# Sliding-window attention into a SwiGLU block: transposes moved from TensorE to DMA, denominators by ones columns, first two FFN tiles interleaved

## The chip, the cores and the metric

One core of a Trainium2 chip. The metric is the device time of one execution, in microseconds (us). A run counts as fast when it is within 1.5% of the fastest of the same kernel. The granted clock is the share of TensorE's full clock that the profile records as granted. "SP" is the SyncE queue, which issues DMAs in program order; "ACT" is ScalarE, "DVE" VectorE, "PE" TensorE, "POOL" GpSimd.

## The reference

```python
def attention(q, k, v):                    # each [8 batches, 8 heads, 576, 64]
    scores = q @ k.T / sqrt(64)
    # query i sees keys i-63 .. i only
    attn = softmax(where((rel >= 0) & (rel < 64), scores, -1e9))
    return attn @ v

def reference(q, k, v, w_gate, w_val, w_out):
    x = attention(q, k, v)                 # as [4608 tokens, 512 channels]
    g = x @ w_gate                         # [512, 1536]
    return (silu(g) * (x @ w_val)) @ w_out # [1536, 512]
```

## The kernel before

The 4608 tokens are cut into 9 tiles t of 512. A tile has 4 units: unit u = 4t + p is a pair of heads, and needs loads of q, k and v, transposed queries and keys (channels on partitions), scores, exponentials, a mask, products with the values, and a division by the softmax denominators. A stage w = 4t + s does a quarter of the FFN of tile t (three gate/value blocks, and a quarter of the output projection of tile t-1) and, from w = 4, attention work some units ahead. Per unit:

```python
def casts(u):                  # GpSimd: f32 -> bf16
    nc.gpsimd.tensor_copy(q_b[:], ...); nc.gpsimd.tensor_copy(k_b[:], ...)
    nc.gpsimd.tensor_copy(vb[0:64, p, :, 0:64], v_f[0:64]); ...
def transposes(u):             # TensorE, then copies out of PSUM
    for i, x in enumerate((q_b, k_b)):
        for c in range(4):
            nc.tensor.transpose(tp[:, i, P * c:P * c + P], x[:, c, :], identb[:])
    nc.scalar.copy(qT[:], tp[:, 0, :])
    nc.vector.tensor_copy(kb[0:64, p, :, 0:64], kt[0:64])        # block-diagonal keys
    nc.vector.tensor_copy(kb[64:128, p, :, 64:128], kt[64:128])
def products(u):
    for j in range(-1, 8):
        nc.tensor.matmul(o_ps[:, lo:hi], vb, Ef[:, e0:e0 + hi - lo], ...)   # channels x queries
    for c in range(2):                                                      # denominators
        nc.tensor.matmul(d_ps[:], bones[:], E[:, :, c, :], ...)
    nc.vector.reciprocal(r[:], d_ps[:])                                     # 128 x 512
    nc.vector.tensor_mul(xT[t][:, p, :], o_ps[:], r[:])
```

The even part of the schedule:

```python
    for w in range(NU):
        # ... (w < 4 is the start)
        gate_value(t, 3 * s)
        products(w + 4)
        gate_value(t, 3 * s + 1)
        transposes(w + 5)
        project(t - 1, s, ps_o, "o")      # ends with a store by SP
        load(w + 8)                       # all loads by SP
        casts(w + 6)
        scores(w + 5)
        gate_value(t, 3 * s + 2)
```

Loads of a unit are split where a tile crosses a batch (576 is not a multiple of 512): 6 DMAs a unit at the first and last tile, 12 at the other even tiles, up to 20 at odd tiles, each with 256-byte rows.

The softmax here doesn't subtract the row's maximum and nothing guards it: scores larger than these inputs give would overflow.

## Time and profile before

| | before |
|---|---|
| median of 3 runs | 470.54 us (470.15 to 472.04) |
| PE, DVE busy | 78%, 72% |
| period of a stage in the even part | 11.5 us |
| period of a stage without attention, near the end | 7.8 us |

The page's busy times of the kernel before, and its chain of waits (the work that ended last, followed back), by engine and by line:

```profile
PE 367.7 (78%) x2332; PEld 189.3 (40%) x2332; DVE 338.8 (72%) x380; ACT 145.2 (31%) x253; POOL 176.9 (38%) x258
...
DVE 52%; PE 35%; ACT 4%; SPq 3%; issue 2%; POOL 2%; DMA 1%; DVEq 0%; POOLq 0%; ACTq 0%
DVE r L217 24%; PE g_ps L229 14%; PE v_ps L229 9%; DVE hT L237 9%; DVE sg L236 8%; PE o_ps L242 6%; DVE xT L218 5%; PE s_ps L175 4%; ACT th L234 3%; SPq L88 2%; POOL E L183 2%; DVE kbd_93 L153 1%; DVE kbd_94 L153 1%; DVE kbd_93 L152 1%; PE ad_ps L215 1%
```

Neither engine is full, yet the chain runs mostly through DVE. The window of one stage of before gives each engine's busy time in it (columns: window, length, busy time and instructions by engine, granted clock, DMA share, GB/s):

```profile
core 0: us, PE busy (x) PEld busy (x) DVE busy (x) ACT busy (x) POOL busy (x), PEclk, DMA share, GB/s
245.20:256.70 11.50, 9.69 (x67) 5.04 (x65) 8.71 (x12) 3.99 (x7) 4.71 (x8) 1.00 0.32 79
```

So PE has 1.8 us a stage without work, and DVE 2.8 us. Where PE waits is seen in the timeline of a stage of before (columns: start, length, engine, line, operation, tile; in brackets the idle time before it and what ended it):

```profile
302.81 3.35 DVE L217 RECIPROCAL r<-ad_ps 128x512 f32<-128x512 f32 x1
...
308.19 0.41 DVE L152 COPY kbd_93<-tp 64x512 bf16<-64x512 bf16 x1
308.61 0.43 DVE L153 COPY kbd_93<-tp 64x512 bf16<-64x512 bf16 x1
...
309.10 0.37 PE L175 MATMUL s_ps<-qT,kbd_93 128*128 128x128 bf16 x4 [1.81 <-DVE kbd_93 L153]
```

The key copies stand behind the reciprocal in DVE's order, and the score matmuls stand behind the key copies. The list of PE's waits of before adds these up:

```profile
PE s_ps L175 <- DVE kbd_93 L153: 31.6, 16, 4.8
PE s_ps L175 <- DVE kbd_94 L153: 29.2, 15, 2.7
```

The last view of before is the SP queue in a stage with an odd tile's loads:

```profile
229.62 4.49 SPq L88 DMA_DIRECT2D q_f<-in_q_dram  x8
234.20 4.44 SPq L88 DMA_DIRECT2D k_f<-in_k_dram  x8
238.74 2.61 SPq L95 DMA_DIRECT2D v_f<-in_v_dram  x4
241.45 1.56 SPq L248 DMA_DIRECT2D out_dram<-os__2519  x1
```

In this view a query or key load takes on average 0.56 us of SP's time to issue, and a value load, to 64 partitions, 0.65 us, short gaps included. The size hardly matters: over the whole trace, 64-partition value loads of two rows a partition hold SP 0.61 us (median), those of eight rows, four times the bytes, 0.63 us. The 20 loads take 11.5 us here and the store 1.56 us (0.54 us in the stage before it).

### The profile page before, as it was taken

How to read it: one execution, taken by the hardware profiler on the slowest of the kernel's cores; microseconds unless marked ns; L12 is line 12 of the kernel's file. 1: busy time of each engine (PE TensorE's matmuls, PEld its weight loads, DVE VectorE, ACT ScalarE, POOL GpSimd, SP SyncE). 2: the span in 40 equal slices, each digit the busy share in tenths (PEclk: the TensorE clock that was granted, in tenths of full speed). 3: DMA queues.
4: the chain of work that ended last, by engine and by line, in shares of the span. 5: the costliest groups of instructions: out<-in, count | busy, mean ns of one | idle time of the engine just before them, and what ended most of it. 6: DMA issues, size and time to landing. Idle time of an engine off the chain costs nothing.

```text
span 468.9 us, 6826 instructions
## 1 busy us (share of the span) xinstructions
PE 367.7 (78%) x2332; PEld 189.3 (40%) x2332; DVE 338.8 (72%) x380; ACT 145.2 (31%) x253; POOL 176.9 (38%) x258
## 2 busy tenths in 40 slices
PE   1453866738888888888888888888888888889996
PEld 0331433414444444444444444444444444444443
DVE  7188798777777777777777777777777777776540
ACT  1220222313333333333333333333333333323232
POOL 3873445424444444444444444444444433110000
PEclk9975897879999999999999999999999999999999
DMA  7965567741332355333333443233343330001012
GB/s 173 253 182 130 154 183 209 219 104 46 87 87 67 79 138 124 87 76 82 87 86 92 119 111 90 70 90 92 90 113 92 91 89 24 22 24 45 22 46 89
DMA packets 129314, 47.65 MB, mean 102 GB/s; under 512 B 119040, under 2 KB 123136, under 8 KB 129280
## 3 DMA queue, kind: packets, MB, share of 16 engines
q1 hardware_dynamic: 129280, 47.22, 39.3%
q8 instruction: 18, 0.29, 0.3%
q14 instruction: 16, 0.13, 0.1%
HBM read 37.75 MB, written 9.44 MB: 101 GB/s over the span
## 4 chain that ended last, share of the span: by engine, by line
DVE 52%; PE 35%; ACT 4%; SPq 3%; issue 2%; POOL 2%; DMA 1%; DVEq 0%; POOLq 0%; ACTq 0%
DVE r L217 24%; PE g_ps L229 14%; PE v_ps L229 9%; DVE hT L237 9%; DVE sg L236 8%; PE o_ps L242 6%; DVE xT L218 5%; PE s_ps L175 4%; ACT th L234 3%; SPq L88 2%; POOL E L183 2%; DVE kbd_93 L153 1%; DVE kbd_94 L153 1%; DVE kbd_93 L152 1%; PE ad_ps L215 1%
## 5 line engine op out<-in xcount | busy, mean ns | idle before, releaser
L183 POOL TENSOR_TENSOR E<-E,mask 128x512 bf16<-128x512 bf16 (+1 forms) x72 | 84.5, 1185 | 215.4 <-ACT E L180 215.4
L236 DVE SCALAR_TENSOR_TENSOR sg<-th,g_ps 128x512 f32<-128x512 f32 x108 | 73.9, 684 | 86.5 <-ACT th L234 86.4
L217 DVE RECIPROCAL r<-ad_ps 128x512 f32<-128x512 f32 x36 | 120.7, 3353 | 5.0 <-PE ad_ps L215 5.0
L229 PE MATMUL g_ps<-xT,wg 128*128 128x512 bf16 x432 | 115.4, 391 | 2.9 <-DVE xT L218 2.9
L229 PE MATMUL v_ps<-xT,wv 128*128 128x512 bf16 x432 | 114.3, 388 | 0.0
L234 ACT ACTIVATE th<-g_ps 128x512 f32<-128x512 f32 x108 | 64.5, 597 | 128.4 <-PE g_ps L229 128.4
L242 PE MATMUL o_ps<-wo,hT 128*128 128x512 bf16 x432 | 98.6, 379 | 0.0
L237 DVE TENSOR_TENSOR hT<-sg,v_ps 128x512 bf16<-128x512 f32 x108 | 74.2, 687 | 11.6 <-PE v_ps L229 0.6
L229 PEld LDWEIGHTS <-wv 128*128 128x128 bf16 x432 | 43.3, 100 | 57.2 <-issue 8.6
L180 ACT ACTIVATE E<-s_ps 128x512 bf16<-128x512 f32 (+1 forms) x72 | 39.1, 592 | 68.6 <-PE s_ps L175 68.6
L242 PEld LDWEIGHTS <-hT 128*128 128x128 bf16 x432 | 41.1, 98 | 44.6
L229 PEld LDWEIGHTS <-wg 128*128 128x128 bf16 x432 | 40.9, 100 | 44.5 <-issue 3.5
L175 PE MATMUL s_ps<-qT,kbd_93 128*128 128x128 bf16 (+1 forms) x160 | 14.0, 232 | 33.0 <-DVE kbd_93 L153 31.6
L149 ACT COPY qT<-tp 128x512 bf16<-128x512 bf16 x36 | 21.1, 586 | 45.6 <-PE tp L147 45.6
L175 PE MATMUL s_ps<-qT,kbd_94 128*128 128x128 bf16 (+1 forms) x128 | 10.3, 224 | 29.2 <-DVE kbd_94 L153 29.2
L147 PE MATMUL tp<-identb,q_b 128*128 128x128 bf16 x144 | 14.8, 229 | 16.9 <-POOL q_b L108 16.9
L215 PE MATMUL ad_ps<-E,bones 128*128 128x512 bf16 x72 | 23.1, 405 | 5.4 <-DVE r L217 5.4
L175 PEld LDWEIGHTS <-kbd_93 128*128 128x128 bf16 x160 | 10.8, 107 | 39.1 <-DVE kbd_93 L153 36.3
L218 DVE TENSOR_TENSOR xT<-ao_ps,r 128x512 bf16<-128x512 f32 x36 | 24.9, 692 | 1.2
L108 POOL CAST q_b<-q_f 128x512 bf16<-128x512 f32 x36 | 22.7, 630 | 6.1 <-DMA q_f<-in_q_dram 4.5
L109 POOL CAST k_b<-k_f 128x512 bf16<-128x512 f32 x36 | 22.1, 613 | 4.3 <-PE g_ps L229 3.3
L147 PEld LDWEIGHTS <-q_b 128*128 128x128 bf16 x144 | 11.3, 102 | 26.0 <-POOL q_b L108 18.2
(77 smaller groups left out, 240.7 us busy)
## 6 DMA issues: line engine op xcount, KB each, us to landing
w_f<-in_moe_w_gate_dram SPq DMA_DIRECT2D x4, 768.0 KB, 5.4
w_f<-in_moe_w_val_dram SPq DMA_DIRECT2D x4, 768.0 KB, 7.1
q_f<-in_q_dram SPq DMA_DIRECT2D x32, 96.0 KB, 3.8
k_f<-in_k_dram SPq DMA_DIRECT2D x32, 96.0 KB, 2.4
wo_f<-in_moe_w_out_dram SPq DMA_DIRECT2D x4, 768.0 KB, 6.0
q_f<-in_q_dram SPq DMA_DIRECT2D x16, 128.0 KB, 2.8
k_f<-in_k_dram SPq DMA_DIRECT2D x16, 128.0 KB, 3.2
v_f<-in_v_dram SPq DMA_DIRECT2D x16, 128.0 KB, 3.2
```

The costliest lines, as they stand in the source:

```text
L147: nc.tensor.transpose(tp[:, i, P * c:P * c + P], x[:, c, :], identb[:])
L175: nc.tensor.matmul(s_ps[:, 64 + P * i:64 + P * i + n], kbd[t % 2][:, p, j, :], qT[:, 64 * j:64 * j + n],)
L180: nc.scalar.activation(Ef[:, 512 * h + lo:512 * h + 512], s_ps[:, lo:512], AF.Exp, scale=0.125)
L183: nc.gpsimd.tensor_mul(Ef[:, 512 * h + lo:512 * h + 512], Ef[:, 512 * h + lo:512 * h + 512], mask[:].rearrange("r m c x -> r (m c x)")[:, ...
L215: nc.tensor.matmul(d_ps[:], bones[:], E[:, :, c, :], start=(c == 0), stop=(c == 1))
L217: nc.vector.reciprocal(r[:], d_ps[:])
L218: nc.vector.tensor_mul(xT[t][:, p, :], o_ps[:], r[:])
L229: nc.tensor.matmul(ps[:], w[:, c, P * m:P * m + P], xT[t][:, c, :], start=(c == 0), stop=(c == 3),)
L234: nc.scalar.activation(th[:], g_ps[:], AF.Tanh, scale=0.5)
L236: nc.vector.scalar_tensor_tensor(sg[:], th[:], 1.0, g_ps[:], ALU.add, ALU.mult)
L237: nc.vector.tensor_mul(hT[t][:, m, :], sg[:], v_ps[:])
L242: nc.tensor.matmul(o_ps[:], hT[t][:, c, P * s:P * s + P], wo[:, c, :], start=(c == 0), stop=(c == 11),)
```

## The change

Its intent: take the transposes off PE, the copies off ACT and DVE, and the 128x512 reciprocal off DVE. Keys are cast into a tile padded with zeros, so that a DMA transpose writes the block-diagonal form at once. The product is taken the other way round (queries on partitions), with two columns of ones beside the values, so that the denominators come out of the same matmul, four numbers a partition. The output then has to be transposed too, again by DMA. Early loads move to ACT's queue, and the first two FFN tiles are interleaved so that attention has more time to get ahead. (A factor of 0.5 also moves, from the cast of the output weights to the copy of the result.) The diff, cut to its core:

```diff
+    vbd = [... VW = 130 columns: values and two of ones]; kpad = [cst.tile([P, 8, P], BF16 ...) x 2]
-    def casts(u): ...            # GpSimd casts
-    def transposes(u): ...       # 8 TensorE transposes, qT copy on ACT, 2 kbd copies on DVE
+    def turn(u, eng):
+        eng.tensor_copy(kp[0:64, :, 0:64], k_f[0:64])
+        eng.tensor_copy(kp[64:128, :, 64:128], k_f[64:128])
+        nc.sync.dma_start_transpose(out=kbd[t % 2][:, p], in_=kp[:].rearrange("r j x -> r (j x)"))
+        eng.tensor_copy(q_b[:], q_f[:].rearrange("r c h d -> r c (h d)"))
+        nc.sync.dma_start_transpose(out=qT[:], in_=q_b[:].rearrange("r c x -> r (c x)"))
     def products(u):
-        ... 9 matmuls (channels x queries), 2 denominator matmuls
-        nc.vector.reciprocal(r[:], d_ps[:])
-        nc.vector.tensor_mul(xT[t][:, p, :], o_ps[:], r[:])
+        for h in range(2):
+            ... 6 matmuls o_ps[r0:r0 + m, i, :] <- Ef[:, e0:e0 + m], vb      # queries x 130
+            nc.vector.reciprocal(r[:], o_ps[:, :, P:VW])                     # 128 x 4
+            nc.vector.tensor_mul(x_b[...], o_ps[:, :, 0:P], r[...])          # 128 x 256
+        nc.sync.dma_start_transpose(out=xT[t][:, p, :]..., in_=x_b[:]...)
@@ schedule
-    for u in range(4): load(u)                      # SP
+    for u in range(4): load(u, act)                 # ACT's queue; also units 4 to 7 and most weights
+    ... units 4 to 7 between the first FFN blocks; then for s in 1, 2, 3:
+        load(7 + s, sp); two blocks of tile 0; turn(7 + s, pool); ...; scores(7 + s); tile 1 ...; products(7 + s)
     for w in range(8, NU):
         gate_value(t, 3 * s); products(w + 4); gate_value(t, 3 * s + 1)
-        transposes(w + 5); project(t - 1, s, ps_o, "o"); load(w + 8); casts(w + 6); scores(w + 5)
+        scores(w + 5, pool); project(t - 1, s, ps_o, "o"); turn(w + 6, pool); load(w + 8, sp)
         gate_value(t, 3 * s + 2)
```

More of the change, by code (lines that the diff above doesn't have):

```diff
@@ L5 @@
 from concourse import bass_utils, mybir
-from concourse.masks import make_identity
 from concourse._compat import with_exitstack
@@ L38 @@
     NU = NT * 4
+    VW = 130
     ctx.enter_context(tc.manual_schedule())
@@ L56 @@
     kbd = [cst.tile([P, 4, 8, P], BF16, name=f"kbd{i}") for i in range(2)]
-    vbd = [cst.tile([P, 4, 8, P], BF16, name=f"vbd{i}") for i in range(2)]
-    identb = cst.tile([P, P], BF16, name="identb")
-    bones = cst.tile([P, P], BF16, name="bones")
+    vbd = [cst.tile([P, 4, 8, VW], BF16, name=f"vbd{i}") for i in range(2)]
+    kpad = [cst.tile([P, 8, P], BF16, name=f"kpad{i}") for i in range(2)]
     mask = cst.tile([P, 8, 2, 64], BF16, name="mask")
@@ L72, with load @@
     staged = {}
-    def load(u):
+    def load(u, eng):
         t, p = divmod(u, 4)
         q_f = stage.tile([P, 4, 2, D], FP32, name="q_f", tag="q_f")
-        k_f = stage.tile([P, 4, 2, D], FP32, name="k_f", tag="k_f")
+        k_f = stage.tile([P, 8, D], FP32, name="k_f", tag="k_f")
         v_f = stage.tile([P, 8, D], FP32, name="v_f", tag="v_f")
-        for dst, src in ((q_f, q), (k_f, k)):
-            for off, b, s0, n in segments(t):
-                o, s, left = off, s0, n
-                while left:
-                    if o % P or left < P:
-                        m, r = 64, 64
-                    else:
-                        m, r = left // P * P, P
-                    for a in range(2):
-                        nc.sync.dma_start(
-                            dst[o % P:o % P + r, o // P:o // P + max(1, m // P), a, :],
-                            src[b, 2 * p + a, s:s + m].rearrange("(c r) d -> r c d", r=r),
-                        )
-                    o, s, left = o + m, s + m, left - m
         for off, b, s0, n in segments(t):
             for a in range(2):
-                nc.sync.dma_start(
+                eng.dma_start(
+                    k_f[64 * a:64 * a + 64, off // 64:(off + n) // 64],
+                    k[b, 2 * p + a, s0:s0 + n].rearrange("(j r) d -> r j d", r=64),
+                )
+        for off, b, s0, n in segments(t):
+            o, s, left = off, s0, n
+            while left:
+                if o % P or left < P:
+                    m, r = 64, 64
+                else:
+                    m, r = left // P * P, P
+                for a in range(2):
+                    eng.dma_start(
+                        q_f[o % P:o % P + r, o // P:o // P + max(1, m // P), a, :],
+                        q[b, 2 * p + a, s:s + m].rearrange("(c r) d -> r c d", r=r),
+                    )
+                o, s, left = o + m, s + m, left - m
+        for off, b, s0, n in segments(t):
+            for a in range(2):
+                eng.dma_start(
                     v_f[64 * a:64 * a + 64, off // 64:(off + n) // 64],
@@ L99, in load @@
         staged[u] = (q_f, k_f, v_f)
-    ready = {}
-    def casts(u):
+    queries = {}
+    def turn(u, eng):
         t, p = divmod(u, 4)
         q_f, k_f, v_f = staged.pop(u)
+        kp = kpad[u % 2]
+        eng.tensor_copy(kp[0:64, :, 0:64], k_f[0:64])
+        eng.tensor_copy(kp[64:128, :, 64:128], k_f[64:128])
+        nc.sync.dma_start_transpose(
+            out=kbd[t % 2][:, p], in_=kp[:].rearrange("r j x -> r (j x)")
+        )
         q_b = cast.tile([P, 4, P], BF16, name="q_b", tag="q_b")
-        k_b = cast.tile([P, 4, P], BF16, name="k_b", tag="k_b")
-        nc.gpsimd.tensor_copy(q_b[:], q_f[:].rearrange("r c h d -> r c (h d)"))
-        nc.gpsimd.tensor_copy(k_b[:], k_f[:].rearrange("r c h d -> r c (h d)"))
+        eng.tensor_copy(q_b[:], q_f[:].rearrange("r c h d -> r c (h d)"))
+        qT = att.tile([P, 4, P], BF16, name="qT", tag="qT")
+        nc.sync.dma_start_transpose(out=qT[:], in_=q_b[:].rearrange("r c x -> r (c x)"))
         vb = vbd[t % 2]
@@ L112, in casts, with weights_gv @@
         nc.gpsimd.tensor_copy(vb[64:128, p, :, 64:128], v_f[64:128])
-        ready[u] = (q_b, k_b)
+        queries[u] = qT
     raw = {}
-    def weights_gv(s):
+    def weights_gv(s, eng):
         for i, src in enumerate((moe_w_gate, moe_w_val)):
             w_f = wst.tile([P, 4, 384], FP32, name="w_f", tag="w_f")
-            nc.sync.dma_start(
+            eng.dma_start(
                 w_f[:], src[:, 384 * s:384 * s + 384].rearrange("(c r) f -> r c f", r=P)
@@ L127, in casts_gv, with weights_o @@
             nc.vector.tensor_copy(dst[:, :, 384 * s:384 * s + 384], raw.pop((i, s))[:])
-    def weights_o(s):
+    def weights_o(s, eng):
         w_f = wst.tile([P, 3, DM], FP32, name="wo_f", tag="w_f")
-        nc.sync.dma_start(
+        eng.dma_start(
             w_f[:], moe_w_out[384 * s:384 * s + 384].rearrange("(c r) f -> r c f", r=P)
@@ L136, in casts_o, with scores @@
     def casts_o(s):
-        nc.vector.tensor_scalar_mul(wo[:, 3 * s:3 * s + 3, :], raw.pop((2, s))[:], 0.5)
-    queries = {}
-    def transposes(u):
+        nc.vector.tensor_copy(wo[:, 3 * s:3 * s + 3, :], raw.pop((2, s))[:])
+    weights = {}
+    def scores(u, eng):
         t, p = divmod(u, 4)
-        q_b, k_b = ready.pop(u)
-        tp = ps_a.tile([P, 2, 512], BF16, name="tp", tag="a")
-        for i, x in enumerate((q_b, k_b)):
-            for c in range(4):
-                nc.tensor.transpose(tp[:, i, P * c:P * c + P], x[:, c, :], identb[:])
-        qT = att.tile([P, 512], BF16, name="qT", tag="qT")
-        nc.scalar.copy(qT[:], tp[:, 0, :])
-        kb = kbd[t % 2]
-        kt = tp[:, 1, :].rearrange("r (j x) -> r j x", x=64)
-        nc.vector.tensor_copy(kb[0:64, p, :, 0:64], kt[0:64])
-        nc.vector.tensor_copy(kb[64:128, p, :, 64:128], kt[64:128])
-        queries[u] = qT
-    weights = {}
-    def scores(u):
-        t, p = divmod(u, 4)
-        qT = queries.pop(u)
+        qT = queries.pop(u)[:].rearrange("r c x -> r (c x)")
         E = att.tile([P, 8, 2, 64], BF16, name="E", tag="E")
@@ L182, in scores @@
             )
-            nc.gpsimd.tensor_mul(
+            eng.tensor_mul(
                 Ef[:, 512 * h + lo:512 * h + 512],
@@ L195, in products @@
         t, p = divmod(u, 4)
-        E = weights.pop(u)
-        Ef = E[:].rearrange("r m c x -> r (m c x)")
+        Ef = weights.pop(u)[:].rearrange("r m c x -> r (m c x)")
         if p == 0:
             xT[t] = xpool.tile([P, 4, 512], BF16, name="xT", tag="xT")
-        o_ps = ps_a.tile([P, 512], FP32, name="ao_ps", tag="a")
-        first = True
-        for j in range(-1, 8):
-            if j < 0 and t == 0:
-                continue
-            vb = vbd[t % 2][:, p, j, :] if j >= 0 else vbd[(t - 1) % 2][:, p, 7, :]
-            lo, hi = max(0, 64 * j), min(512, 64 * j + P)
-            e0 = 64 * (2 * j + 1) if j >= 0 else 0
-            nc.tensor.matmul(
-                o_ps[:, lo:hi], vb, Ef[:, e0:e0 + hi - lo],
-                start=first, stop=(j == 7), skip_group_check=True,
-            )
-            first = False
@@ L213, in products @@
-        d_ps = ps_a.tile([P, 512], FP32, name="ad_ps", tag="a")
-        for c in range(2):
-            nc.tensor.matmul(d_ps[:], bones[:], E[:, :, c, :], start=(c == 0), stop=(c == 1))
-        r = att.tile([P, 512], FP32, name="r", tag="r")
-        nc.vector.reciprocal(r[:], d_ps[:])
-        nc.vector.tensor_mul(xT[t][:, p, :], o_ps[:], r[:])
+        x_b = att.tile([P, 4, P], BF16, name="x_b", tag="x_b")
+        for h in range(2):
+            o_ps = ps_a.tile([P, 2, VW], FP32, name="ao_ps", tag="a")
+            for i in range(2):
+                c = 2 * h + i
+                parts = [(2 * c, 0, P, P * 2 * c + 64), (2 * c + 1, 64, 64, P * (2 * c + 1) + 64)]
+                if c > 0 or t > 0:
+                    parts.append((2 * c - 1, 0, 64, P * 2 * c))
+                for n, (j, r0, m, e0) in enumerate(parts):
+                    vb = vbd[t % 2][:, p, j, :] if j >= 0 else vbd[(t - 1) % 2][:, p, 7, :]
+                    nc.tensor.matmul(
+                        o_ps[r0:r0 + m, i, :], Ef[:, e0:e0 + m], vb,
+                        start=(n == 0), stop=(n == len(parts) - 1), skip_group_check=True,
+                    )
+            r = att.tile([P, 2, 2], FP32, name="r", tag="r")
+            nc.vector.reciprocal(r[:], o_ps[:, :, P:VW])
+            nc.vector.tensor_mul(
+                x_b[:, 2 * h:2 * h + 2, :].rearrange("r c (a d) -> r c a d", a=2),
+                o_ps[:, :, 0:P].rearrange("r c (a d) -> r c a d", a=2),
+                r[:].unsqueeze(3).to_broadcast([P, 2, 2, D]),
+            )
@@ L220 @@
+        nc.sync.dma_start_transpose(
+            out=xT[t][:, p, :].rearrange("r (c x) -> r c x", x=P),
+            in_=x_b[:].rearrange("r c x -> r (c x)"),
+        )
     hT = {}
@@ L246, in project @@
         os_ = fsb.tile([P, 512], FP32, name="os_", tag="os_")
-        nc.scalar.copy(os_[:], o_ps[:])
+        nc.scalar.activation(os_[:], o_ps[:], AF.Copy, scale=0.5)
         nc.sync.dma_start(out[512 * t + P * s:512 * t + P * s + P, :], os_[:])
+    dve, pool, act, sp = nc.vector, nc.gpsimd, nc.scalar, nc.sync
     for u in range(4):
-        load(u)
-    weights_gv(0)
-    load(4)
-    for i in range(2):
-        nc.vector.memset(kbd[i][:], 0.0)
-    make_identity(nc, identb[:])
-    for i in range(2):
-        nc.vector.memset(vbd[i][:], 0.0)
-    casts(0)
-    nc.vector.memset(bones[:], 0.0)
-    nc.vector.memset(bones[0:64, 0:64], 1.0)
-    nc.vector.memset(bones[64:128, 64:128], 1.0)
-    nc.vector.memset(mask[:], 1.0)
+        load(u, act)
+    weights_gv(0, act)
+    for kp in kpad:
+        dve.memset(kp[:], 0.0)
+    for vb in vbd:
+        dve.memset(vb[:], 0.0)
+        for a in range(2):
+            dve.memset(vb[64 * a:64 * a + 64, :, :, P + a:P + a + 1], 1.0)
+    dve.memset(mask[:], 1.0)
     for a in range(2):
         half = mask[64 * a:64 * a + 64]
-        nc.gpsimd.affine_select(
+        pool.affine_select(
             out=half[:, :, 0, :], in_=half[:, :, 0, :], compare_op=ALU.is_ge, fill=0.0,
@@ L270 @@
         )
-        nc.gpsimd.affine_select(
+        pool.affine_select(
             out=half[:, :, 1, :], in_=half[:, :, 1, :], compare_op=ALU.is_ge, fill=0.0,
@@ L274 @@
         )
-    transposes(0)
-    casts(1)
-    weights_gv(1)
-    transposes(1)
-    scores(0)
-    load(5)
-    casts(2)
-    transposes(2)
-    scores(1)
+    turn(0, dve)
+    turn(1, dve)
+    load(4, act)
+    scores(0, dve)
+    turn(2, dve)
+    load(5, act)
     products(0)
-    casts(3)
-    transposes(3)
-    scores(2)
+    scores(1, dve)
+    turn(3, dve)
+    load(6, act)
     products(1)
+    scores(2, dve)
+    load(7, act)
+    weights_gv(1, act)
     casts_gv(0)
-    scores(3)
@@ L293 @@
     products(2)
+    scores(3, dve)
+    turn(4, dve)
     products(3)
-    casts(4)
-    for w in range(NU):
-        t, s = divmod(w, 4)
-        if w < 4:
-            gate_value(t, 3 * s)
-            transposes(w + 4)
-            if w < 2:
-                weights_gv(w + 2)
-            else:
-                weights_o(2 * w - 4)
-                weights_o(2 * w - 3)
-            load(w + 6)
-            casts(w + 5)
-            gate_value(t, 3 * s + 1)
-            if w < 3:
-                casts_gv(w + 1)
-            scores(w + 4)
-            gate_value(t, 3 * s + 2)
-            products(w + 4)
-            if w == 3:
-                for i in range(4):
-                    casts_o(i)
-                load(10)
-                load(11)
-                transposes(8)
-                casts(9)
-                scores(8)
-            continue
+    scores(4, dve)
@@ new lines @@
+    turn(5, dve)
+    gate_value(0, 0)
+    products(4)
+    scores(5, dve)
+    turn(6, dve)
+    gate_value(0, 1)
+    weights_gv(2, act)
+    products(5)
+    scores(6, dve)
+    turn(7, dve)
+    gate_value(0, 2)
+    casts_gv(1)
+    products(6)
+    scores(7, dve)
+    weights_gv(3, act)
+    products(7)
+    for s in range(1, 4):
+        load(7 + s, sp)
+        gate_value(0, 3 * s)
+        gate_value(0, 3 * s + 1)
+        turn(7 + s, pool)
+        if s == 1:
+            casts_gv(2)
+            weights_o(0, sp)
+            weights_o(1, sp)
+        if s == 2:
+            casts_gv(3)
+            weights_o(2, sp)
+            weights_o(3, sp)
+        gate_value(0, 3 * s + 2)
+        if s == 1:
+            for m in range(3):
+                gate_value(1, m)
+        scores(7 + s, pool)
+        gate_value(1, 3 * s)
+        gate_value(1, 3 * s + 1)
+        products(7 + s)
+        if s == 3:
+            for i in range(4):
+                casts_o(i)
+        gate_value(1, 3 * s + 2)
@@ L326 @@
+    load(11, sp)
+    turn(11, pool)
+    load(12, sp)
+    project(0, 0, ps_o, "o")
+    scores(11, pool)
+    turn(12, pool)
+    load(13, sp)
+    project(0, 1, ps_o, "o")
+    products(11)
+    turn(13, pool)
+    load(14, sp)
+    project(0, 2, ps_o, "o")
+    scores(12, pool)
+    load(15, sp)
+    project(0, 3, ps_o, "o")
+    for w in range(8, NU):
+        t, s = divmod(w, 4)
         gate_value(t, 3 * s)
@@ L330 @@
         if w + 5 < NU:
-            transposes(w + 5)
+            scores(w + 5, pool)
         project(t - 1, s, ps_o, "o")
+        if w + 6 < NU:
+            turn(w + 6, pool)
         if w + 8 < NU:
-            load(w + 8)
-        if w + 6 < NU:
-            casts(w + 6)
-        if w + 5 < NU:
-            scores(w + 5)
+            load(w + 8, sp)
         gate_value(t, 3 * s + 2)
```

## The prediction

> **What bounds it now.** In the even middle part (stages of 11.50 us, windows of one stage) TensorE is busy 9.69 us, VectorE 8.71, ScalarE 4.0, GpSimd 4.7; the granted clock is full. A stage without attention, near the end, takes 7.77 us: the FFN's 36 matmuls at 216 ns. The timeline of a stage shows the loss: VectorE's 3.35 us reciprocal stands in front of the key copies, so TensorE idles about 1.8 us (list of waits: score matmuls wait for kbd). The chain of waits alternates VectorE (52%, reciprocal 24%) and TensorE (35%). The first FFN tile starts at about 43 us, stage 4 at about 108 us; the clock is below 0.9 between.
>
> **Taken away, per unit (36 units).** 8 TensorE transposes (about 0.5 us) and 2 denominator matmuls (0.43 us); the reciprocal (now 2 tiny ones) and two key copies (0.41 and 0.43 us) on VectorE; the 0.59 us query copy on ScalarE. The xT multiply (0.69 us) becomes two halves. TensorE should need about 9.0 us a stage, VectorE about 5.3 (4.1 of it the FFN). Alone, that makes the even part TensorE-bound at about 9.1 us: 2.4 us x 28 stages = 67 us off.
>
> **Added, and where it hurts.** Three DMA transposes per unit (256 KB keys with zeros, 128 KB queries, 128 KB output) go in order into the SP queue. It is already almost full: the timeline shows each load issue taking 0.555 us (64-row ones 0.65), 20 loads and a store in 10 to 11 us of an 11.5 us stage at odd tiles. The change has 12 loads (even tiles) or 16 (odd), 8 to 10 us with the store. So SP, not TensorE, sets the pace: about 9.1 us + S, S being how long a unit's transposes hold SP. No trace here has one. The Trainium skill, "DMA: Bandwidth & Descriptors", section Latency and other measured facts, gives 261 GB/s for transposes, 2 us for 512 KB; "VectorE: DVE Perf Modes", section The three transpose paths, gives 1309 ns for one 128x128, 21 us if 16 went one by one. If SP is held only for the issue, S is about 1.7 us (3 x 0.56); if until they are moved at 261 GB/s, 3 us or more.
>
> Start: loads of units 4 to 7 are issued by ScalarE in front of its exponentials, about 8.4 us each, so the first gate matmul should come at 55 to 60 us. From there SP owes about 352 loads (206 us), 36 stores and 28 units' transposes: by estimate 430 us in all for S = 1.7, 470 us for S = 3, 520 us for S = 5. I weigh the small S more, since the design moves early loads off SP to leave it to the transposes.
>
> **Prediction: 445 us, range 408 to 525 (8 in 10).** Faster by over 2%: 0.57; within 2%: 0.12; slower: 0.31.
>
> **What would show it.** Reciprocal gone from the chain of waits; TensorE near 9.0 us busy per even stage; VectorE under 6 us; SP queue busy nearly always, even-tile stages shorter than odd-tile ones; last attention stages near 9.1 us; end stages still 7.77 us. First gate matmul after 50 us. Score matmuls waiting for qT or kbd by DMA where SP is late. DMA share up from about 0.35 to 0.6 or more.
>
> **What would make it wrong.** Transposes that move slowly or hold SP for several us each: every stage is SP's and the kernel clearly slower. Or transposes that cost SP next to nothing, and stages of 9.1 us throughout: 400 to 415 us. Also transpose latency at tile borders, when the FFN waits for xT.

## The result

The changed kernel is slower: 562.75 us median of 3 (559.54 to 565.88) against 470.54 us; ratio 1.195, interval 1.183 to 1.207. Ratios here are the mean time of one kernel's fast runs over that of the other's of the same rounds, so not quite the ratio of the medians quoted. Output is correct.

The page of the changed kernel, same lines as above:

```profile
PE 397.6 (71%) x2080; PEld 183.8 (33%) x2080; DVE 223.1 (40%) x421; ACT 126.2 (22%) x217; POOL 165.0 (29%) x252
...
PE 48%; DMA 20%; SPq 17%; DVE 4%; ACTq 3%; issue 3%; ACT 2%; POOL 2%; POOLq 0%; DVEq 0%
PE o_ps L243 15%; PE g_ps L230 13%; DMA qT<-q_b 11%; PE v_ps L230 11%; SPq L94 5%; PE ao_ps L205 5%; SPq L82 4%; DMA v_f<-in_v_dram 3%; SPq L101 3%; SPq L116 3%; PE s_ps L171 2%; DMA xT<-x_b 2%; DMA k_f<-in_k_dram 2%; ACTq L101 1%; ACT th L235 1%
```

DVE's work fell by a third (338.8 to 223.1 us), and the reciprocal left the chain. But SP's issues and DMAs now make up 37% of the chain, where they had been 4%. PE's waits of the changed kernel say for what:

```profile
PE s_ps L167 <- DMA qT<-q_b: 83.6, 21, 13.5
PE ao_ps L205 <- DVE E L179: 40.5, 4, 19.0
PE g_ps L230 <- DMA xT<-x_b: 18.0, 5, 5.5
PE s_ps L171 <- DMA qT<-q_b: 15.1, 1, 15.1
```

The score matmuls wait for transposed queries, 99 us in all: 60 us before w = 8, and 37 us from w = 8 to 24. The second line, 40.5 us for the masked exponentials E, lies in the first 66 us of the run (see 9). One whole stage of SP's queue of the changed kernel, with an even tile's loads:

```profile
355.13 0.52 SPq L249 DMA_DIRECT2D out_dram<-os__2664  x1
355.74 1.30 SPq L116 DMA_TRANSPOSE kbd_94<-kpad_98  x1
357.14 1.21 SPq L122 DMA_TRANSPOSE qT<-q_b  x1
358.40 2.61 SPq L82 DMA_DIRECT2D k_f<-in_k_dram  x4
361.05 2.13 SPq L94 DMA_DIRECT2D q_f<-in_q_dram  x4
363.22 2.59 SPq L101 DMA_DIRECT2D v_f<-in_v_dram  x4
365.91 1.23 SPq L216 DMA_TRANSPOSE xT<-x_b  x1
367.24 0.52 SPq L249 DMA_DIRECT2D out_dram<-os__2789  x1
```

There is no gap over 0.15 us: SP sets the pace. This holds for the whole middle part: counted over the trace from w = 8 to 24, the gaps over 0.2 us between SP's entries add up to 1.1 us of 230.2 us, where in the kernel before they made 23.6 of 184.5 us. The seven entries of one stage add up to 11.6 us and the period is 12.1 us (367.24 - 355.13). Three transposes take 1.30 + 1.21 + 1.23 = 3.74 us of it. With 16 loads, at odd tiles, the period is 14.9 us. How long a transpose takes to land is in the list of DMA issues of the changed kernel (last number: median us from issue to landing):

```profile
qT<-q_b SPq DMA_TRANSPOSE x36, 2.5
xT<-x_b SPq DMA_TRANSPOSE x36, 2.5
kbd_93<-kpad_97 SPq DMA_TRANSPOSE x10, 3.3
```

When SP has few loads left to issue (w from 24), the changed kernel shows the stage that was hoped for:

```profile
core 0: us, PE busy (x) PEld busy (x) DVE busy (x) ACT busy (x) POOL busy (x), PEclk, DMA share, GB/s
460.80:470.40 9.60, 9.60 (x59) 4.72 (x58) 5.17 (x11) 3.47 (x6) 5.34 (x8) 1.00 0.74 156
```

PE is full at 9.60 us. Note that this is only 0.09 us less work for PE than the 9.69 us of before.

PE's waits also cost clock. The same 12 projection matmuls of the changed kernel, after a wait of 2.4 us for qT and in a stage without one (same columns):

```profile
261.00:265.30 4.30, 4.30 (x14) 1.61 (x12) 0.00 (x0) 0.97 (x2) 3.56 (x5) 0.60 0.44 99
285.70:288.60 2.90, 2.90 (x18) 1.37 (x16) 0.69 (x1) 1.17 (x3) 2.10 (x2) 1.00 0.45 100
```

The granted clock is 0.60 in the first, and the projection takes 4.4 us instead of 2.75. The Trainium skill, "TensorE: Matmul & The Clock Gate", Part 1, describes this ("activity releases the throttle"); the trace agrees, with a mean clock of 0.89 after against 0.96 before (0.85 against 1.00 between w = 8 and 24).

Where the 92 us arose, by the start of the output projection of a stage on PE (read from the timelines; "end" is the span):

| part | before | after | difference |
|---|---|---|---|
| until w = 8 | 154.6 us | 212.4 us | +57.8 |
| w = 8 to 24 (the changed kernel's SP issues 12 to 16 loads a stage) | 184.5 | 230.2 | +45.7 |
| w = 24 to 31 (few or no loads) | 80.3 | 68.6 | -11.7 |
| w = 31 to the end | 49.5 | 49.7 | +0.2 |

So two things are to be explained: the middle, 2.9 us a stage slower on average, and the start. The stage w = 8 alone took 23.7 us, against 11.5 us before, so 12 of the 45.7 us lie at the head of the middle.

### The profile page after: what moved, and what is told of

The parts are those of the page before. It is cut to its first block, busy times and chain, and to the rows that moved or that the text cites. A ratio compares the mean times of both kernels' runs of the same rounds, so it can differ in the third digit from the quotient of the medians.

```text
span 561.0 us, 6420 instructions
## 1 busy us (share of the span) xinstructions
PE 397.6 (71%) x2080; PEld 183.8 (33%) x2080; DVE 223.1 (40%) x421; ACT 126.2 (22%) x217; POOL 165.0 (29%) x252
## 4 chain that ended last, share of the span: by engine, by line
PE 48%; DMA 20%; SPq 17%; DVE 4%; ACTq 3%; issue 3%; ACT 2%; POOL 2%; POOLq 0%; DVEq 0%
PE o_ps L243 15%; PE g_ps L230 13%; DMA qT<-q_b 11%; PE v_ps L230 11%; SPq L94 5%; PE ao_ps L205 5%; SPq L82 4%; DMA v_f<-in_v_dram 3%; SPq L101 3%; SPq L116 3%; PE s_ps L171 2%; DMA xT<-x_b 2%; DMA k_f<-in_k_dram 2%; ACTq L101 1%; ACT th L235 1%
## 5 line engine op out<-in xcount | busy, mean ns | idle before, releaser
L230 PE MATMUL v_ps<-xT,wv 128*128 128x512 bf16 x432 | 121.3, 407 | 0.0
L179 POOL TENSOR_TENSOR E<-E,mask 128x512 bf16<-128x512 bf16 x56 | 63.6, 1151 | 180.7 <-ACT E L176 180.7
L243 PE MATMUL o_ps<-wo,hT 128*128 128x512 bf16 x432 | 115.1, 423 | 0.4 <-DVE wo L150 0.2
L205 PE MATMUL ao_ps<-vbd_95,E 128*64 128x130 bf16 (+1 forms) x236 | 35.5, 257 | 40.5 <-DVE E L179 40.5
L205 PEld LDWEIGHTS <-E 128*64 128x64 bf16 (+1 forms) x428 | 30.8, 107 | 74.0 <-DVE E L179 41.5
L167 PE MATMUL s_ps<-qT,kbd_93 128*128 128x64 bf16 x36 | 7.7, 214 | 47.2 <-DMA qT<-q_b 46.8
L167 PE MATMUL s_ps<-qT,kbd_94 128*128 128x64 bf16 x32 | 6.7, 210 | 37.5 <-DMA qT<-q_b 36.7
L211 DVE TENSOR_TENSOR x_b<-ao_ps,r 128x256 bf16<-128x256 f32 x72 | 30.6, 425 | 2.5
L179 DVE TENSOR_TENSOR E<-E,mask 128x512 bf16<-128x512 bf16 (+1 forms) x16 | 6.7, 417 | 57.6 <-ACT E L176 35.4
L205 PE MATMUL ao_ps<-vbd_96,E 128*64 128x130 bf16 (+1 forms) x192 | 28.8, 254 | 0.2 <-POOL E L185 0.2
L171 PE MATMUL s_ps<-qT,kbd_93 128*128 128x128 bf16 (+1 forms) x160 | 15.1, 246 | 15.1 <-DMA qT<-q_b 15.1
L167 PEld LDWEIGHTS <-kbd_93 128*128 128x128 bf16 x36 | 3.9, 109 | 52.9 <-DMA qT<-q_b 51.3
```

The lines of the kernel that those rows point to most:

```text
L171: nc.tensor.matmul(s_ps[:, 64 + P * i:64 + P * i + n], kbd[t % 2][:, p, j, :], qT[:, 64 * j:64 * j + n],)
L179: eng.tensor_mul(Ef[:, 512 * h + lo:512 * h + 512], Ef[:, 512 * h + lo:512 * h + 512], mask[:].rearrange("r m c x -> r (m c x)")[:, lo:512],)
L205: nc.tensor.matmul(o_ps[r0:r0 + m, i, :], Ef[:, e0:e0 + m], vb, start=(n == 0), stop=(n == len(parts) - 1), skip_group_check=True,)
L211: nc.vector.tensor_mul(x_b[:, 2 * h:2 * h + 2, :].rearrange("r c (a d) -> r c a d", a=2), o_ps[:, :, 0:P].rearrange("r c (a d) -> r c a d" ...
L230: nc.tensor.matmul(ps[:], w[:, c, P * m:P * m + P], xT[t][:, c, :], start=(c == 0), stop=(c == 3),)
L243: nc.tensor.matmul(o_ps[:], hT[t][:, c, P * s:P * s + P], wo[:, c, :], start=(c == 0), stop=(c == 11),)
```

## The experiments

All ran with 3 rounds, beside the kernel before (470.8 to 471.8 us), all with correct output. The times of the experiments are medians of 4 runs. Where the text below gives the time of a stage of an experiment, it is from store to store in SP's queue or from projection to projection on PE. "w = 8" and "middle" (w = 8 to 24) are read as in the table above.

| kernel | time | ratio to before | w = 8 | middle |
|---|---|---|---|---|
| before | 470.5 | 1 | 154.6 | 184.5 |
| changed | 562.8 | 1.195 | 212.4 | 230.2 |
| changed, keys and queries in one transpose | 548.4 | 1.162 | 213.0 | 213.5 |
| changed, query loads by ACT | 533.4 (529.4 for the two fast runs) | 1.122 | 213.1 | 200.0 |
| changed, loads one unit earlier | 544.0 | 1.154 | 198.5 | 228.3 |
| changed, units 4 to 7 loaded by SP | 564.6 | 1.196 | 214.4 | 229.0 |
| changed, units 4 to 7 by SP and ACT | 558.1 | 1.184 | 207.7 | 229.7 |
| changed, units 4 to 7 loaded late | 571.9 | 1.211 | 226.1 | 227.7 |
| changed, all repairs | 495.3 | 1.049 | 180.6 | 197.0 |
| changed, all repairs, ACT's issues spread | 487.3 | 1.036 | 186.5 | 179.0 |
| before, with three idle transposes a unit | 516.6 | 1.095 | 154.8 | 221.8 |
| before, ones columns, all transposes on PE | 435.5 | 0.922 | 142.4 | 171.2 |
| the same, output transposed by DMA | 486.6 | 1.030 | 171.2 | 191.6 |
| before, reordered | 432.3 | 0.918 | 146.9 | 167.4 |
| before, reordered, value loads by ACT | 484.1 | 1.021 | 157.4 | 206.8 |

The theory (A) was that SP's in-order queue sets the pace, because each transpose holds it for about 1.25 us; rivals are named in each.

### 1. Keys and queries in one transpose

```diff
-        nc.sync.dma_start_transpose(out=kbd[t % 2][:, p], in_=kp[:]...)      # 256 KB
-        nc.sync.dma_start_transpose(out=qT[:], in_=q_b[:]...)                # 128 KB
+        nc.sync.dma_start_transpose(out=kq[t % 2][:, p], in_=kp[:]...)       # 12 blocks, 384 KB
```

> The changed kernel, but each unit's keys (256 KB) and queries (128 KB) go through one DMA transpose instead of two; result correct. Theory A (each transpose instruction holds SP for a fixed 1.2 to 1.3 us, whatever its size): the merged record lasts 1.3 to 1.5 us, SP's work falls by about 1.3 us a unit, the even-tile stage falls from 12.1 us to about 10.8 us, the whole kernel to 515 to 535 us. Rival B (SP is held in proportion to the bytes or blocks moved): the merged record lasts 2.4 to 2.6 us and the kernel stays at 550 to 565 us.

A stage of SP's queue in this run:

```profile
355.45 1.23 SPq L215 DMA_TRANSPOSE xT<-x_b  x1
356.78 0.52 SPq L248 DMA_DIRECT2D out_dram<-os__2717  x1
357.41 1.48 SPq L118 DMA_TRANSPOSE kq<-kpad  x1
358.94 2.85 SPq L83 DMA_DIRECT2D k_f<-in_k_dram  x4
```

The transpose of 384 KB holds SP for 1.48 us, three times the bytes of the 1.23 us one: the hold is nearly fixed per instruction, as theory A had it. The gain was smaller than forecast, 548.4 us instead of 515 to 535: stages with 12 loads took 11.4 to 12.1 us instead of 10.8. The key loads behind the longer transpose took 2.85 us instead of 2.61, and it lands after 3.8 us instead of 2.5 (from the list of DMA issues), so that SP and PE may wait more for each other; that this is where the rest of the gain went is not shown. The landing does grow with size: 2.5, 3.3 and 3.8 us for 128, 256 and 384 KB, by estimate 128 KB in 0.65 us, about 200 GB/s, on top of some 1.9 us.

### 2. Query loads by ACT in the even part

```diff
-            load(w + 8, sp)
+            load(w + 8, sp, act)          # k and v by SP, q by ACT
```

> The changed kernel, but in the even part (w from 8) the query loads are issued by ScalarE's queue; transposes untouched, result correct. Theory A (SP's issue order is the pace): the even-tile stage goes from 12.1 to about 10.0 us, the odd-tile stage from 14.9 to about 10.2 us, in all about 50 us off: 505 to 520 us. Rival B (the DMA engines or the latency of the transposes are the pace, not who issues): stages stay at 12 and 15 us and the time within 10 us of 562.

533.4 us, and 529.4 us for the two fast runs: 33 us off, fast runs compared, and the middle went from 230.2 to 200.0 us. So who issues does matter, with the transposes untouched, which speaks against rival B. But the forecast of 505 to 520 us was missed. Stages with four query loads on ACT came to 10 to 11 us between SP's stores, those with eight stayed at 12.1 to 14.5 us: eight issues in a row on ACT delay its tanh (shown more plainly under 4).

### 3. Loads one unit earlier in the interleaved part

```diff
+    load(8, sp)
     for s in range(1, 4):
-        load(7 + s, sp)
         gate_value(0, 3 * s); gate_value(0, 3 * s + 1)
         turn(7 + s, pool)
+        load(8 + s, sp)
```

> The changed kernel, but in the interleaved first two FFN tiles the loads of units 8 to 11 are issued one unit earlier, so that a unit's casts don't follow directly on its own loads. Theory A (the ramp is a serial chain: output transpose in SP, then 7.3 us of loads, landing, casts, transposes, scores, mask, products, again the output transpose): the period of these units falls from 21 us to 13 to 15 us, the kernel to 535 to 550 us. Rival B (the ramp is bound by TensorE's low clock or by VectorE): period and time unchanged within 1%.

544.0 us, in the forecast range, 19 us off. Of the 16.7 us between the two profiled runs 13.9 us come from the start (w = 8 at 198.5 us instead of 212.4). The output transposes of units 8, 9 and 10, 21 us apart in the changed kernel (124.3, 146.0 and 166.9 us), are 16.6 us apart here, a little more than forecast. The start is in part a serial chain, in which a unit's loads were issued only after the output transpose of the unit before had been through SP.

### 4. All repairs together, and a second form

```diff
# both: one transpose for keys and queries; loads one unit earlier; q by ACT in the even part; units 4 to 7:
-    load(4, act) ... load(7, act)
+    load(4, sp) ... load(7, sp)                       # first form; also q of units 9 to 15 by ACT
+    load(4, sp, act) ... load(7, sp, act)             # second form
# second form: ACT's query issues are kept in a list and issued in twos, between gate_value blocks
```

> The changed kernel with all four repairs together: one transpose for keys and queries, query loads from unit 9 on by ScalarE's queue, loads one unit earlier in the interleaved part, units 4 to 7 loaded by SP. Theory A (everything lost was queue order): even-part stages of 9.6 to 10.2 us and w = 8 reached at about 190 us instead of 230: 455 to 480 us in all, about the time of the kernel before. Rival B (something beside the queues holds the design back): above 500 us.

495.3 us, missed by 15 us, though far from the 562 us. (The 230 us in the forecast is a slip: the changed kernel reached w = 8 at 212.4 us.) The reason is in the timeline of a stage with eight query loads in this run:

```profile
262.42 6.59 ACTq L96 DMA_DIRECT2D q_f<-in_q_dram  x8
...
269.11 1.08 ACT L235 ACTIVATE th<-g_ps 128x512 f32<-128x512 f32 x2 [6.16 <-DMA k_f<-in_k_dram]
...
270.48 1.87 PE L230 MATMUL g_ps<-xT,wg 128*128 128x512 bf16 x4 [3.45 <-DVE sg L237]
```

ACT spends 6.59 us on eight issues, two tanh wait behind them, and PE idles 3.45 us. Not all of the 6.59 us is issuing: the trace's single entries show 1.78 us of waiting before the eighth issue (the reason is under 9). Hence the second form:

> The version with all repairs, with two differences: ScalarE's query loads are issued in twos between its other work instead of up to eight in a row, and the loads of units 4 to 7 are divided between SP and ScalarE. Theory A (in the version with all repairs, eight issues in a row, 5 to 6.6 us, kept tanh waiting at odd tiles): stages at tile 3 (w = 12 to 15) fall from 15.5 to 9.6 to 11 us, the kernel from 495 to 455 to 475 us. Rival B (something else, as GpSimd or transpose latency, makes odd tiles slow): these stages stay above 14 us and the time above 485 us.

487.3 us: the stages named fell from 15.5 to 10 to 12 us, and the middle to 179.0 us, 5.5 us less than before's. So that part of the theory held. The total missed its range, because w = 8 was reached at 186.5 us, 32 us later than in the kernel before. What the even part had lost is thereby accounted for by what stands in the queues, its number and its order; the start is not repaired.

### 5. Before, with three idle transposes a unit

```diff
             load(w + 8)
+            for jk, n in zip(junk, (8, 4, 4)):         # scratch that nothing reads
+                nc.sync.dma_start_transpose(out=jk[:], in_=mf[:, 0:P * n])
```

> The kernel before, with three DMA transposes of a constant tile (256, 128 and 128 KB, into scratch tiles that nothing reads) put into the SP queue after the loads of each stage w = 4 to 31; everything else as before, result correct. Theory A (a transpose costs SP about 1.25 us of issue): SP needs about 16 us in stages with 20 loads and about 11 us in those with 12, so the loads fall behind at odd tiles; two stages of prefetch (about 20 us) hide a part, the time rises from 471 to 480 to 505 us with nothing waiting on the transposes' data. Rival B (what hurt was waiting for transposed data, not the queue): within 1% of 471 us.

516.6 us, more than forecast. SP's queue of this run, in a stage with 20 loads:

```profile
163.93 4.47 SPq L89 DMA_DIRECT2D q_f<-in_q_dram  x8
168.50 4.46 SPq L89 DMA_DIRECT2D k_f<-in_k_dram  x8
173.06 3.17 SPq L96 DMA_DIRECT2D v_f<-in_v_dram  x4
176.27 3.96 SPq L339 DMA_TRANSPOSE junk<-mask  x3
```

Three transposes whose data nobody waits for hold SP 3.96 us and make the stage 17.0 us by SP. This is the cost by itself: adding them to the kernel before costs 45 us, 37 of it between w = 8 and 24, where the changed kernel loses 46. The idle transposes also move data, and the DMA share there rose from 0.38 to 0.54, which this run does not separate; but SP's gaps over 0.2 us add up to only 1.2 of 221.8 us, so its queue was full. It also shows that before had little room in SP: prefetch hid less than the 20 us I had counted on.

### 6. Before, with ones columns and all transposes on PE

```diff
     def products(u):          # as in the changed kernel: queries x 130 columns, reciprocal 128 x 4
-        nc.sync.dma_start_transpose(out=xT..., in_=x_b...)
+    def turn_out(u):
+        for c in range(4): nc.tensor.transpose(xp[:, P * c:P * c + P], x_b[:, c, :], identb[:])
+        nc.scalar.copy(xT[t][:, p, :], xp[:])
```

> The kernel before with one part of the change alone: output queries by channels with ones columns for the denominators (no 512-wide reciprocal, no denominator matmuls), output transposed back by TensorE; queries and keys as before, no DMA transpose. Theory A (before is held by the reciprocal in front of VectorE's other work): stage falls from 11.5 us to 9.7 to 10.1 us, TensorE-bound, kernel 410 to 430 us. Rival B (the reciprocal only fills time that VectorE had to spare): stage stays above 11 us and time above 455 us.

435.5 us, 8% faster than before: one half of the change, done alone, is a gain. A stage takes 10.25 us with PE full (10.25 us busy in a window of 10.30), a little above the forecast range: twelve matmuls of 130 columns with a new stationary operand each take 1.35 us, where before's nine took about 0.45 us (from the timelines, from the first of the group to what follows).

### 7. The same, with only the output transposed by DMA

```diff
-        for c in range(4): nc.tensor.transpose(...)      ; nc.scalar.copy(...)
+        nc.sync.dma_start_transpose(out=xT[t][:, p, :]..., in_=x_b[:]...)
```

> The version with ones columns and TensorE transposes (435.5 us), with one thing changed: the output (128 KB a unit) is transposed by one DMA transpose in the SP queue instead of four TensorE transposes and a ScalarE copy. Theory A (1.25 us more in SP, and the transpose waits in order behind up to 20 loads): stages with 12 loads fall from 10.25 to about 10.0 us, stages with 20 loads need about 13.5 us of SP and the FFN waits for xT at tile borders: 443 to 465 us. Rival B (a DMA transpose that takes over work of a busy TensorE is worth it): 425 to 433 us.

486.6 us: one DMA transpose a unit, in place of 0.22 us of PE, costs 51 us, more than forecast. PE's longest waits in this run:

```profile
PE g_ps L240 <- DMA xT<-x_b: 59.4, 14, 13.6
```

Here it is less the 1.25 us that hurts than the place in the queue: the output transpose stands behind up to 20 loads in SP, the FFN needs it at the tile border, and PE waits up to 13.6 us. In stages with 12 loads the period was 10.03 us, as forecast.

### 8. Before, reordered

```diff
         gate_value(t, 3 * s)
+        transposes(w + 5)
         products(w + 4)
         gate_value(t, 3 * s + 1)
-        transposes(w + 5)
```

> The kernel before with one move and nothing else: from w = 4 on, a unit's TensorE transposes and key copies stand ahead of the products and the reciprocal of the unit before it. Theory A (before loses its 1.8 us a stage because the key copies wait in VectorE's order behind the 3.35 us reciprocal, not because VectorE is full: 8.7 of 11.5 us): stage falls to 9.7 to 10.3 us, TensorE-bound, kernel 420 to 440 us, as good as the version with ones columns. Rival B (VectorE's amount of work is what counts): stage stays above 11 us, time above 455 us.

432.3 us, with ones columns on PE (435.5 us) the fastest; the intervals of their ratios overlap, 0.915 to 0.921 and 0.918 to 0.925. The 3.36 us reciprocal is still there; the key copies merely stand in front of it (timeline of this run):

```profile
303.01 0.41 DVE L152 COPY kbd<-tp 64x512 bf16<-64x512 bf16 x1
303.44 0.43 DVE L153 COPY kbd<-tp 64x512 bf16<-64x512 bf16 x1
303.89 3.36 DVE L217 RECIPROCAL r<-ad_ps 128x512 f32<-128x512 f32 x1
...
307.32 0.36 PE L175 MATMUL s_ps<-qT,kbd 128*128 128x128 bf16 x4
```

A stage takes 9.55 us, and PE no longer waits before the scores. This is the 9.6 us that the changed kernel reaches only where SP has few loads. What before lost in its even part it lost to order, not to an amount of work.

PE's waits for query casts (17.2 us in four waits) were then taken for waits at tile borders, and the 20 loads of SP's stages at odd tiles (12.5 to 13 us) for their cause. So the value loads went to ACT:

```diff
-                nc.sync.dma_start(
+                (nc.scalar if u >= 12 else nc.sync).dma_start(
                     v_f[...], v[...])
```

> The reordered kernel before (432 us) with one more thing: from unit 12 on, the four value loads of a unit are issued by ScalarE. Theory A (at odd tiles its stages of 12.5 to 13 us are SP's 20 loads and a store, and TensorE waits there for the query casts): odd-tile stages fall to 9.6 to 10.5 us, the kernel to 410 to 424 us. Rival B (odd tiles are slow by GpSimd or VectorE): these stages stay above 12 us, the time within 1% of 432 us.

484.1 us, fifty worse than the reordered kernel, and 1.4 to 2.9% slower than before (by the 2% rule unclear): neither theory. The middle's stages slowed to 11.3 to 14.9 us. The four issues (2.6 to 4.7 us on ACT) stand in front of the exponentials, and the products then wait for the mask (37 us of PE's waits). The forecast also rested on a misreading: the four waits for query casts all lie in the first 25 us of the run, here (17.3 us) as in before (16.9 us), and not at tile borders.

What holds the reordered kernel is seen in its own trace. From w = 8 to 24 only four of its 16 stages take over 10 us, w = 8 and 9 (13.3 us each), 16 and 17 (10.9 and 14.9 us), and SP's gaps over 0.2 us add up to 2.6 of 167.4 us, so its queue is nearly full there. At w = 17 (GpSimd casts keys and masks E in one order, and PE waits for the mask):

```profile
247.67 0.61 POOL L109 CAST k_b<-k_f 128x512 bf16<-128x512 f32 x1 [5.44 <-DMA v_f<-in_v_dram]
250.57 2.25 POOL L183 TENSOR_TENSOR E<-E,mask 128x512 bf16<-128x512 bf16 x2
251.77 0.36 PE L208 MATMUL ao_ps<-E,vbd 128*128 128x64 bf16 x4 [2.62 <-POOL E L183]
```

The mask stands behind casts that waited for loads, which were late after four SP stages of 20 loads. So the loads are on the path of these stages; that fewer of them would cure it, no run shows.

### 9. The start

The first gate matmul comes at 73.6 us in the changed kernel and at 40.8 us in before. In between, ACT issues loads of units 4 to 7 in front of its exponentials, and PE waits 40.5 us for the masked exponentials of units 0 to 3. Three runs asked whether that is the reason. First, all four units by SP:

```diff
-    load(4, act)        # and 5, 6, 7, each at its place between the steps of units 0 to 3
+    load(4, sp)
```

> The changed kernel, but units 4 to 7 are loaded by SP instead of ScalarE, at the same places of the program. Theory A (ScalarE's own issues stand in front of its exponentials in the start, 8 to 10 us for each of four units): the first gate matmul comes at 62 to 67 us instead of 73.6 us, the kernel at 545 to 555 us. Rival B (the start is bound by the whole number of issues, on whichever queue): first gate matmul not before 72 us, time unchanged within 1% of 562 us.

No gain: first gate matmul at 74.9 us, 564.6 us in all. The theory as put there fell. Then divided between SP and ACT (`load(4, sp, act)`):

> The changed kernel, with the loads of units 4 to 7 divided: keys and values from SP, queries from ScalarE. Moving them all to SP had changed nothing. Theory A2 (the start is bound by the number of issues in any one in-order queue: about 9 us of loads a unit on either, plus 3.8 us of transposes on SP): with the work divided the first gate matmul comes at 56 to 66 us instead of 73.6, the kernel at 545 to 556 us. Rival B2 (the start is bound by the chain of latencies from load to output transpose, not by issue): first gate matmul not before 71 us, time within 1% of 562 us.

First gate matmul at 70.5 us, 558.1 us in all: nearer to the rival's numbers than to the theory's. In this run ACT's six query issues of unit 4 lasted 8.86 us instead of 5.17 us in the changed kernel. In the built program each DMA waits for one of eight numbered DMA semaphores (counters that tell when an earlier DMA has landed), dealt out in program order over both queues, so an issue on ACT can wait for an earlier DMA of SP to land. The trace shows this: of the 8.86 us, 5.75 us are waits before the second, third and fourth issue, which start at 24.42, 26.30 and 30.62 us, each 0.02 or 0.03 us after a DMA of SP on the same semaphore landed (24.40, 26.27 and 30.60 us). The 1.78 us under 4 are the same: the eighth issue starts at 268.66 us, and SP's transpose on its semaphore landed at 268.64. How much of the whole start this costs, no run tests. Last, the loads of units 4 to 7 moved behind the products of unit 3:

```diff
     products(3)
+    for u in range(4, 8):
+        load(u, sp)
     turn(4, dve)
```

> The changed kernel, but units 4 to 7 are loaded only after the products of unit 3, by SP; a diagnosis, not meant to be faster. Theory A3 (units 0 to 3 take until 71 us because loads of the next units stand among their steps in the in-order queues, and moving them from one queue to another can't help, since DMAs of both queues wait for shared semaphores in the order of the program): the last output transpose of unit 3 is issued at 32 to 45 us instead of 69.6. Rival B3 (the chain of a unit, casts, transposes, scores, mask, products, output transpose, is that slow by itself): not before 60 us. Whole time: 540 to 575 us either way, as the same loads then delay units 4 to 7.

SP's queue of this run:

```profile
31.07 1.19 SPq L122 DMA_TRANSPOSE qT<-q_b  x1
32.35 9.94 SPq L216 DMA_TRANSPOSE xT<-x_b  x3
42.35 1.22 SPq L82 DMA_DIRECT2D k_f<-in_k_dram  x2
```

Units 1 to 3 have their output transposes issued by 42.3 us, instead of 69.6 us: the units' own chain is not slow, the loads between its steps are. But SP then spends 42 to 78 us on the four units' loads, and the first gate matmul comes at 83.3 us. I read from the three runs that it is the sum of loads and transposes in order that fills the start, and that moving it about does little. This is argued and not shown: no run takes any of them away.

## Why the prediction was wrong

- **What bounds before.** Right in what it named: the key copies behind the reciprocal, PE idle 1.8 us a stage. But it did not ask whether this wait could go without removing the reciprocal. The reordered kernel shows that moving it suffices (432.3 us).
- **"S is about 1.7 us (3 x 0.56) ... I weigh the small S more."** This is the first step that failed, and the term of the sum that was mis-sized: S measured 3.74 us. A transpose holds SP for 1.2 to 1.3 us, 2.2 times a load, nearly independent of its bytes. The mechanism, that SP and not PE sets the pace, was right and is shown by the full queue, by the query loads moved to ACT and by the idle transposes in before. The prediction's own figures (430 us for 1.7, 470 for 3, 520 for 5) give about 490 us for 3.74, so this step leads from the forecast 445 us to 490 us and leaves 73 us to the start (next point). My reason for the small S, that the design moves early loads off SP to leave it to the transposes, was no evidence about the chip.
- **"The first gate matmul should come at 55 to 60 us."** The second step that failed: 73.6 us, and w = 8 at 212.4 us, 57.8 us behind before. I costed the issues but not the chain between them: loads, transposes and output transposes of consecutive units wait for each other in order. The sum let SP issue without pause from the first gate matmul on; between it (73.6 us) and w = 8 SP in fact stood idle 42 of 139 us (gaps over 0.2 us in the trace). By estimate the 490 us, some 16 us of later start and these 42 us make about 550 of the 562.75 us. Loading one unit earlier gave back 14 us of the start.
- **"TensorE should need about 9.0 us a stage."** Mis-sized: 9.60 us. The 0.93 us saved was real, but the twelve 130-column matmuls cost about 0.9 us more (1.35 against 0.45 us) than the nine they replace, which the sum left out. So even with a free queue the design had almost nothing to win over a well-ordered before (9.60 against 9.55 us).
- **VectorE under 6 us, the end stages at 7.77 us, the reciprocal gone from the chain, scores waiting for qT.** Right: 5.17 us, 7.8 us, and the waits as shown. The last attention stages took 9.6 us, not 9.1, and the DMA share between w = 8 and 24 was 0.52, not 0.6 or more.
- **Latency at tile borders**, named as a risk: 18 us of PE's waits for xT, a small part of the loss; in experiment 7 it was the main one.
- **Chances.** Faster had 0.57. From the two figures of the skill that I quoted, the transfer would by estimate take 2 us (512 KB at 261 GB/s) to 21 us (16 blocks of 1309 ns one by one); neither speaks of the issue, and the odds leaned on the kinder one.

What stays open: how much of the start can be won back within this design (the best form reached w = 8 at 180.6 us, before at 154.6, so 32 of the 57.8 us came back), how much the shared semaphores have in it, and what part of it belongs to the interleaved schedule alone, since no run has that schedule with the transposes on PE. Nor does a run relieve SP in the reordered kernel without loading ACT.

## What to carry to other kernels

Before replacing an operation, look at what stands in front of what in each in-order queue: two lines moved gave 8% here, while the large change that removed the same operation lost 20%. Work moved "to DMA" is moved to the queue that issues it; count that queue's entries, because here each cost a nearly fixed time whatever its bytes (0.5 to 0.65 us a load, 1.2 to 1.5 us a transpose), and a result needed soon stands behind whatever was issued before it. Another engine's queue is free only if nothing urgent follows the issues there; here it helped to issue in small groups. Look also at what each issue waits for: with shared semaphores it was a DMA of the other queue.

## What the Trainium skill lacked or had wrong

- "DMA: Bandwidth & Descriptors", section Issuing engines are not separate DMA queues, says that issuing from several engines only saves the sequencer's time, "which is usually small relative to the DMA itself". In this kernel it is the pace: 0.53 to 0.65 us a load and 1.2 to 1.5 us a transpose fill SP's queue, while the DMA engines' mean share is 0.52 between w = 8 and 24; moving the query loads to ACT gained 33 us. The skill does have this case elsewhere: "Perfetto Trace Analysis", section What "DMA-bound" means, counts an issuing queue that is solid with DMA entries among the bounds.
- The same page gives the transfer rate of a DMA transpose (section Latency and other measured facts: 261 GB/s with a non-contiguous middle dimension) but no time, measured on this chip, for which one holds the issuing queue; the issue times that it has stand in a comparison of a trn3 form with "previous generations". Here it was 1.21, 1.30 and 1.48 us for 128, 256 and 384 KB. The landing times of 2.5, 3.3 and 3.8 us give about 200 GB/s by difference, an estimate below the page's figure, with about 1.9 us on top.
- "VectorE: DVE Perf Modes", section The three transpose paths, sets 1309 ns for one 128x128 DMA transpose beside 390 ns on TensorE. Sixteen blocks a unit in three DMAs took 3.74 us of issue and land in 2.5 to 3.3 us each here, so the time does not add up by blocks; and four TensorE transposes in a row took 0.39 us of busy time, so the table's ratio of the two paths doesn't carry over to either.
- No page warns that DMA issues on ScalarE's queue delay its activations: eight issues took 4.7 to 7.1 us there (experiments 2 and 4, waits included), and in one such stage PE idled 3.45 us behind them.
